# Loads moved to other places in the order, keys in whole rows, and 64 bytes between the squares and the weights

## The chip, the cores and the metric

The kernel runs on one core of one Trainium2 chip. A core has five engines with a queue each: TensorE (PE; the loading of its stationary operand is shown apart, as PEld), VectorE (DVE), ScalarE (ACT), GpSimd (POOL) and SyncE (SP), which here issues every transfer. The engines work in the order of their own queues and wait for each other through semaphores. The metric is the time of one execution on the device in microseconds (us); lower is better.

## The reference

Attention with a local window and block summaries, and a feed-forward layer behind it, all in float32:

```python
k_sum = k.reshape(B, H, nb, block, D).max(axis=3)      # B, H, S, D = 4, 8, 768, 64; block 32
v_sum = v.reshape(B, H, nb, block, D).mean(axis=3)     # nb = 24
scores_l = scale * q @ k^T, kept where |i - j| < 16, else -1e9
scores_s = scale * q @ k_sum^T + log(32)
a = softmax([scores_l, scores_s])
attn = a @ [v, v_sum]
x = attn as 3072 tokens x 512
out = square(max(x @ w_in, 0)) @ w_out                 # 512 -> 2048 -> 512
```

## The kernel before

**Groups and chunks.** The 3072 tokens are 24 groups `g` of 128 (six to a batch, `NT = 6`); group `g` belongs to batch `g // 6`. Two groups make a chunk `c` of 256 tokens, and there are 12 chunks. The feed-forward layer of a chunk walks the 2048 hidden features in 16 blocks of 128, two to a slot.

**The feed-forward layer.** Every float32 operand is split in a high and a low part of type float32r, and a product is made of three: high by high, low weights by high, high weights by low. `ffn1` (L391) makes 12 matmuls for one block: the stationary operand is a piece of the weights `w_sb[f]`, the moving one is `xh` or `xl`, 256 columns. `squares` applies ReLU (ACT, L399), the high square `gh` (ACT, L405), the product (DVE, L410) and the low square `gl` (DVE, L413). `ffn2` (L432) makes 6 matmuls for one block: the stationary operand is a piece of the squares `gh_sb` or `gl_sb`, the moving one is 512 columns of `w_sb[f]`. A slot, so, is 24 matmuls of L391 and 12 of L432; the second product of a slot comes after the first product of the next slot (`finish`).

**Attention's visits.** While TensorE works on chunk `c`, the softmax of the groups of the next chunk runs on DVE, ACT and POOL. `period(a)` lists that work for the groups `a` and `a + 1` over eight slots; each slot has three lists, `before` and `after` the squares and `last`. At the end of its eighth list, `last[7]`, stands what this text calls a visit: TensorE leaves the feed-forward layer and makes `outputs(a)` and `outputs(a + 1)` (L361, 32 matmuls) and then `scores_by_group(a + 2)` (L278, 128 matmuls, for two groups). `split_x` then makes `xh` and `xl` of the next chunk. One slot of the running chunk follows the visit before the next chunk begins.

**Loads.** All transfers are issued by SP, in the order of the program. `load_v` (L139), `load_q` (L125) and `load_k` (L131, L132) of the groups to come stand in `last[7]`, right behind the visit in the order: values for `a + 2` and `a + 3`, queries and keys for `a + 4` and `a + 5`. As SP has its own queue, it issues them as soon as the buffers are free, which two matmul groups of the visit decide: `outputs` for the values, `scores_by_group` for the queries and keys. Buffers go by `g % 2`. `load_kv` (L175, L176) brings whole rows of keys and values of the next batch, out of which `sum_k` (L179) and `sum_v` (L184, L187) make the block maxima and means on DVE; it stands in `last[0]` and `last[3]`, the sums two slots later.

**The keys' layout.** In `k_sb` a row (one partition) holds 8 runs of 120 elements: 64 keys, the 24 block maxima, 32 keys. A load fills the keys of each run (256 bytes and 128 bytes a piece, two transfers) and leaves the 24 maxima alone. `place_k` (L191) copies the maxima out of `ksum` on DVE, four times in the opening and once for each of two groups at the turn of a batch; the copy then serves the batch.

**Memory.** Tiles of the pool `const` lie one after the other in the order of the code, then the pool `big` with 17 rooms of 8192 bytes a partition (the weights, and the rows of `load_kv` in the one spare), then `work` with three `nmx` and three `sm` tiles of 32 bytes each, `xh`, `xl` and the output tiles. `gh_sb` and `gl_sb` (4096 bytes each) are the last of `const`, so that they begin a whole multiple of 256 bytes before every room of the weights.

**The order.** The string `START` is the order of the opening, written by hand, up to about 140 us; behind it `slot` and `period` give it for the chunks 2 to 11. No planner moves anything.

Of the kernel before, what the change touches and what calls it, by code (L numbers as in the profile page):

```python
# [11 lines left out]
F32 = mybir.dt.float32  # L12
# [5 lines left out]
ALU = mybir.AluOpType  # L18
AX = mybir.AxisListType

B, H, S, D = 4, 8, 768, 64
BLOCK, WINDOW = 32, 16
NB = S // BLOCK
DM, DF = 512, 2048
P = 128
NT = S // P
NPAIR = H // 2
# [6 lines left out]
NK = 96 + NB  # L34
GQ = 32
GK = 64 + NB
FROM_GROUPS = 6
# [36 lines left out]
def attn_ffn_kernel(ctx: ExitStack, tc: tile.TileContext, q, k, k0, kt, v, vt, v0, w, masks, gmasks, ident, mean, out):  # L74
    nc = tc.nc
    scale = 1.0 / math.sqrt(D)

    const = ctx.enter_context(tc.tile_pool(name="const", bufs=1))
# [14 lines left out]
    k_sb = [const.tile([P, 2 * NPAIR * NK], F32, name=f"k_sb{i}") for i in range(2)]  # L93
# [4 lines left out]
    def by_pair(g):  # L98
        return k_sb[g % 2].rearrange("a (s p k) -> a s p k", s=2, p=NPAIR)
# [4 lines left out]

    e_sb = const.tile([P, H, P], F32, name="e_sb")
    pT = [const.tile([P, H, P], F32, name=f"pT{i}") for i in range(2)]
    ksum = const.tile([P, NPAIR, NB], F32, name="ksum")
    vsum = const.tile([P, NPAIR, 32], F32, name="vsum")
    r_sb = const.tile([P, 2, CT], F32, name="r")
    gh_sb = const.tile([P, 4, CT], F32R, name="gh")  # L110
    gl_sb = const.tile([P, 4, CT], F32R, name="gl")


    bank = [ps_s.tile([P, DM], F32, name=n, tag=f"{n}{i}") for i, n in enumerate(["s_ps"] * 4 + ["ph"] * 2)]
# [12 lines left out]
    def load_k(g):  # L127
        if g < FROM_GROUPS:
            nc.sync.dma_start(out=by_run(g)[:, 0:4], in_=k0[g - FROM_KT])
        else:  # L130
            nc.sync.dma_start(out=by_pair(g)[:, :, :, 0:64], in_=k[g // NT, g % NT][:, :, :, 0:64])  # L131
            nc.sync.dma_start(out=by_pair(g)[:, :, :, GK:], in_=k[g // NT, g % NT][:, :, :, 64:])  # L132

    def load_qk(g):
        load_q(g)
        load_k(g)

    def load_v(g):
        nc.sync.dma_start(out=v_sb[g % 2][0:96], in_=v[g // NT, g % NT])  # L139
# [21 lines left out]
    kv, padded = {}, {}  # L161
# [11 lines left out]
    def load_kv(b, p):  # L173
        kv[b, p] = r = room(F32, "kv")
        nc.sync.dma_start(out=r[:, 0:S], in_=kt[b, p])  # L175
        nc.sync.dma_start(out=r[:, S : 2 * S], in_=vt[b, p])  # L176

    def sum_k(b, p):
        nc.vector.tensor_reduce(  # L179
            out=ksum[:, p], in_=kv[b, p][:, 0:S].rearrange("a (n j) -> a n j", j=BLOCK), op=ALU.max, axis=AX.X  # L180
        )

    def sum_v(b, p):
        nc.vector.tensor_reduce(  # L184
            out=vsum[:, p, 0:NB], in_=kv[b, p][:, S : 2 * S].rearrange("a (n j) -> a n j", j=BLOCK), op=ALU.add, axis=AX.X
        )
        nc.vector.tensor_scalar_mul(vsum[:, p, 0:NB], vsum[:, p, 0:NB], 1.0 / BLOCK)  # L187

    def place_k(g):
        dst = by_run(g)[:, 4] if g < FROM_GROUPS else by_pair(g)[:, :, :, 64:GK]  # L190
        nc.vector.tensor_copy(out=dst, in_=ksum.unsqueeze(1).to_broadcast([P, 2, NPAIR, NB]))  # L191

    def place_v(g):
        dst = v_sb[g % 2][96:128]
# [88 lines left out]
    def scores_kt(g, p0, p1):  # L283

        if g not in s_ps:
            s_ps[g] = [bank[r].rearrange("a (p k) -> a p k", p=NPAIR) for r in range(2)]
        for p in range(p0, p1):
            for k0, k1 in ((0, 96), (96, NK)):
                for r, s in ((0, 0), (1, 1), (0, 1), (1, 0)):
                    rs, ss = slice(r * 64, r * 64 + 64), slice(s * 64, s * 64 + 64)  # L290
                    o = g * P + s * 64
                    keys = ksum[rs, p, :] if k0 else padded[p // 2][rs, p % 2, o : o + 96]
                    nc.tensor.matmul(  # L293
                        s_ps[g][r][ss, p, k0:k1], lhsT=q_sb[g % 2][rs, s, p, :], rhs=keys, start=True, stop=True
                    )
# [56 lines left out]
    x_ps = {}  # L352

    def outputs(g):
        xp = bank[2 if g < FROM_GROUPS - 1 else 5 if g < FROM_GROUPS else 5 - g % 2]
        x_ps[g] = xp = xp.rearrange("a (p k) -> a p k", p=NPAIR)

        for s in range(2):
            for h in range(H):
                o = (h % 2) * 64  # L360
                nc.tensor.matmul(  # L361
                    xp[o : o + 64, h // 2, s * 64 : s * 64 + 64],
                    lhsT=v_sb[g % 2][:, s, h * 64 : h * 64 + 64],
                    rhs=pT[g % 2][:, h, s * 64 : s * 64 + 64],
                    start=True, stop=True,
                )
# [13 lines left out]
    def split_x(g):  # L380
        high_x(g)
        low_x(g)
# [71 lines left out]
    n_g = B * NT  # L454
# [28 lines left out]
    def period(a):  # L483

        before, after, last = [[] for _ in range(8)], [[] for _ in range(8)], [[] for _ in range(8)]
        b, t = divmod(a, NT)
        if a >= n_g:  # L490
            return before, after, last
        if b and t == 0:
            after[1] += [lambda: place_v(a), lambda: place_v(a + 1)]
        after[0].append(lambda: softmax(a, 0, 3))
        before[1].append(lambda: softmax(a, 3, 6))
        after[1] += [lambda: softmax(a, 6, 8), lambda: inverse(0), lambda: norm(a, 0, nc.gpsimd)]
        before[2] += [lambda: inverse(1), lambda: norm(a, 1, nc.gpsimd)]
        after[2].append(lambda: turn(a, 0, 3))
        before[3].append(lambda: turn(a, 3, 8))
        after[3].append(lambda: turn(a, 8, 12))  # L500
        before[4].append(lambda: softmax(a + 1, 0, 4))
        after[4].append(lambda: softmax(a + 1, 4, 6))
        before[5] += [lambda: softmax(a + 1, 6, 8), lambda: inverse(0), lambda: norm(a + 1, 0, nc.gpsimd)]
        before[5] += [lambda: inverse(1), lambda: norm(a + 1, 1, nc.gpsimd)]
        before[6].append(lambda: turn(a + 1, 0, 5))
        after[6].append(lambda: turn(a + 1, 5, 8))
        before[7].append(lambda: turn(a + 1, 8, 12))
        if b + 1 < B and t:
            for n, p in enumerate(((0, 1), (2, 3))[t // 4]):
                last[3 * n].append(lambda p=p: load_kv(b + 1, p))  # L510
                after[3 * n + 2].append(lambda p=p: sum_k(b + 1, p))
                after[3 * n + 2].append(lambda p=p: sum_v(b + 1, p))
        if b + 1 < B and t == 4:
            after[6] += [lambda: place_k(a + 2), lambda: place_k(a + 3)]
        last[7] += [lambda: outputs(a), lambda: outputs(a + 1)]
        if a + 2 < n_g:
            last[7].append(lambda: scores_by_group(a + 2))
        last[7] += [lambda: split_x(a), lambda: split_x(a + 1)]
        if a + 2 < n_g:
            last[7] += [lambda g=g: load_v(g) for g in (a + 2, a + 3)]  # L520
        if a + 4 < n_g:
            last[7] += [lambda g=g: load_qk(g) for g in (a + 4, a + 5)]
        return before, after, last


# [3 lines left out]
    free, held = [3, 4, 5], {}  # L529
# [93 lines left out]
    with tc.manual_schedule(engines=None):  # L623
        for token in START.split():
            what, i, j, eng = re.fullmatch(r"(L:[a-z]+|F[12]|[A-Z]+)\.?(\d*)\.?(\d*)([avp]?)", token).groups()
            i, j = int(i or 0), int(j or 0)
# [10 lines left out]
        for c in range(2, n_c):  # L637
            for f in range(0, NF, 2):
                n = (f + 2) // 2 % 8
# [37 lines left out]
def _layouts(q, k, v):  # L677
    qd = q.reshape(B, NPAIR, 2, NT, 2, 64, D).transpose(0, 3, 2, 6, 4, 1, 5)
    kp = np.zeros((B, H, S + 2 * WINDOW, D), k.dtype)
    kp[:, :, WINDOW : WINDOW + S] = k  # L680
    vp = np.zeros((B, H, S + 2 * WINDOW, D), v.dtype)
    vp[:, :, WINDOW : WINDOW + S] = v
    kd = np.zeros((B, NT, 2, D, 2, NPAIR, 96), k.dtype)
    vd = np.zeros((B, NT, 96, 2, H, D), v.dtype)
    for s in range(2):
        for t in range(NT):
            o = t * P + s * 64
            kd[:, t, :, :, s] = kp[:, :, o : o + 96].reshape(B, NPAIR, 2, 96, D).transpose(0, 2, 4, 1, 3)
            vd[:, t, :, s] = vp[:, :, o : o + 96].transpose(0, 2, 1, 3)
    return {  # L690
        "q": np.ascontiguousarray(qd).reshape(B, NT, P, 2, NPAIR, 64),
        "k": kd.reshape(B, NT, P, 2, NPAIR, 96),
        "k0": np.ascontiguousarray(
            kd[0, FROM_KT:].reshape(FROM_GROUPS - FROM_KT, P, 2, NPAIR, 4, NB).transpose(0, 1, 4, 2, 3, 5)
        ),
        "kt": np.ascontiguousarray(k.transpose(0, 1, 3, 2)).reshape(B, NPAIR, P, S),
        "v": vd.reshape(B, NT, 96, 2, DM),
        "vt": np.ascontiguousarray(v.transpose(0, 1, 3, 2)).reshape(B, NPAIR, P, S),
        "v0": np.ascontiguousarray(v[0].reshape(H, NT, P, D).transpose(2, 1, 0, 3)).reshape(P, NT, DM),
    }  # L700
# [24 lines left out]
```

## Time and profile before

| what | value |
|---|---|
| time, median of 3 runs (lowest to highest) | 635.54 us (632.82 to 636.05) |
| the profiled execution: its own time | 633.53 us |
| its span, first to last instruction | 631.7 us |
| TensorE busy (matmul) | 601.6 us, 95% of the span |
| weight load busy | 545.1 us, 86% |
| DVE, ACT, POOL busy | 385.4, 262.5, 88.8 us |
| mean granted TensorE clock | 0.986 |
| moved by DMA | 60.56 MB in 55104 packets |

A busy share says how long an engine had work, not that the work was needed at that time. The chain of waits goes back from the last instruction to what released it, and so on to the start; its pieces are a start, a length and what ran. A piece called issue is time in which the engine waited for nothing that the profile shows. The view by stretches gives, for each stretch of time, the busy time of each engine with its number of instructions, the granted clock of TensorE, the share of the 16 DMA engines in use, and GB/s.

### The profile page before, as it was taken

The page shows a single profiled execution, that of the slowest core. Times are in us where ns is not written, and L with a number is a line of the kernel's source. Part 1 is how long each engine was busy: PE and PEld are TensorE (multiplying, and loading weights), DVE is VectorE, ACT ScalarE, POOL GpSimd, SP SyncE. Part 2 cuts the span into 40 slices and gives each one's busy share as a digit, 9 for nine tenths or more (in the row PEclk, how much of TensorE's full clock was granted, in tenths as well). Part 3 has the DMA queues.
Part 4 walks back from the last instruction along what each step waited for, and adds up shares of the span by engine and source line. Part 5 has one row for each costly group of instructions (what it writes and reads, how often), then busy time and mean ns, then how long its engine had stood idle before and what let it go on. Part 6 is the DMA issues. An engine that isn't in the chain of part 4 may idle for free.

```text
span 631.7 us, 14142 instructions
## 1 busy us (share of the span) xinstructions
PE 601.6 (95%) x5792; PEld 545.1 (86%) x5792; DVE 385.4 (61%) x1077; ACT 262.5 (42%) x690; POOL 88.8 (14%) x83
## 2 busy tenths in 40 slices
PE   3689999999989999999999998999999999999997
PEld 2588889989979999999989988998998998998996
DVE  4889888668535755756644772783763663653221
ACT  3778887332424324424424423334433423332222
POOL 2555663002000000002000000000200000000000
PEclk9879999999999999999999998999999999999999
DMA  8999611553043134123026115205005001000000
GB/s 290 381 341 317 212 71 52 166 164 90 1 111 110 49 87 132 51 76 93 1 58 162 51 38 148 84 1 135 35 1 135 34 0 52 34 2 1 34 1 33
DMA packets 55104, 60.56 MB, mean 96 GB/s; under 512 B 40320, under 2 KB 40448, under 8 KB 52992
## 3 DMA queue, kind: packets, MB, share of 16 engines
q1 hardware_dynamic: 55040, 59.67, 31.5%
q8 instruction: 45, 0.74, 0.5%
q14 instruction: 19, 0.16, 0.1%
HBM read 53.36 MB, written 6.29 MB: 94 GB/s over the span
## 4 chain that ended last, share of the span: by engine, by line
PE 91%; DMA 4%; DVE 2%; issue 1%; SPq 1%; ACT 0%; DVEq 0%
PE ph L391 41%; PE o_ps L432 41%; DMA w_raw<-in_w 4%; PE ph L361 3%; PE s_ps L391 3%; PE s_ps L278 2%; DVE w_raw L236 1%; PE s_ps L361 1%; PE ph L336 0%; PE s_ps L293 0%; PE s_ps L261 0%; DVE w_sb L247 0%; SPq L171 0%; DVE sm L323 0%; ACT w_raw L225 0%
## 5 line engine op out<-in xcount | busy, mean ns | idle before, releaser
L391 PE MATMUL ph<-xh,w_sb 128*128 128x256 f32 x1448 | 264.2, 284 | 2.8 <-issue 2.2
L391 PEld LDWEIGHTS ph<-xh,w_sb 128*128 128x128 f32 x1448 | 228.9, 190 | 10.7 <-issue 2.4
L432 PE MATMUL o_ps<-w_sb,gh 128*128 128x512 f32 x768 | 237.2, 390 | 0.0
L391 PE MATMUL ph<-xl,w_sb 128*128 128x256 f32 x724 | 204.6, 283 | 0.0
L410 DVE TENSOR_TENSOR ph<-ph,r 128x512 f32<-128x512 f32 (+1 forms) x101 | 64.9, 643 | 160.5 <-ACT r L399 159.2
L432 PEld LDWEIGHTS o_ps<-w_sb,gh 128*128 128x128 f32 x768 | 137.3, 188 | 22.8 <-issue 0.2
L432 PE MATMUL o_ps<-w_sb,gl 128*128 128x512 f32 x384 | 149.7, 390 | 0.9 <-DVE gl L413 0.9
L399 ACT ACTIVATE r<-ph 128x512 f32<-128x512 f32 (+1 forms) x91 | 52.0, 571 | 226.0 <-PE ph L391 225.1
L391 PEld LDWEIGHTS ph<-xl,w_sb 128*128 128x128 f32 x724 | 140.1, 194 | 0.0
L314 ACT ACTIVATE e_sb<-e_sb,nmx 128x88 f32<-128x88 f32 (+1 forms) x192 | 69.9, 367 | 71.3 <-DVE nmx L306 71.3
L347 DVE STREAM_TRANSPOSE pT<-e_sb 32x256 f32<-32x256 f32 x216 | 94.1, 436 | 3.4 <-POOL e_sb L330 0.4
L432 PEld LDWEIGHTS o_ps<-w_sb,gl 128*128 128x128 f32 x384 | 72.1, 188 | 16.4 <-DVE gl L413 1.3
L330 POOL TENSOR_TENSOR e_sb<-e_sb,sm 128x352 f32<-128x352 f32 (+1 forms) x43 | 34.7, 810 | 336.4 <-DVE sm L324 198.4
L413 DVE TENSOR_TENSOR gl<-ph,gh 128x512 fp32r<-128x512 f32 (+1 forms) x101 | 64.3, 637 | 10.5 <-DVE ph L410 0.5
L405 ACT ACTIVATE gh<-r 128x512 fp32r<-128x512 f32 (+1 forms) x112 | 64.0, 571 | 9.3 <-DVE r L401 5.8
L240 POOL TENSOR_TENSOR w_raw<-w_raw 128x1024 int32<-128x1024 int32 x16 | 35.6, 2233 | 25.4 <-DVE w_raw L236 8.7
L314 ACT ACTIVATION_READ_ACCUMULATOR e_sb<-e_sb,nmx 128x1 f32 x192 | 36.4, 190 | 0.0
L306 DVE CUSTOM_DVE_ANT_0 e_sb<-s_ps,gmask_sb 128x88 f32<-128x88 f32 x144 | 27.1, 244 | 0.4
L378 DVE TENSOR_TENSOR xl<-ph,xh 128x512 fp32r<-128x512 f32 x19 | 13.1, 691 | 22.4 <-ACT xh L375 22.4
L323 DVE TENSOR_SCALAR sm<-sm 128x4 f32<-128x4 f32 x48 | 13.4, 280 | 16.0 <-ACT e_sb L314 16.0
L375 ACT CAST xh<-ph 128x512 fp32r<-128x512 f32 x19 | 11.1, 587 | 26.6 <-PE ph L361 26.6
L361 PEld LDWEIGHTS ph<-pT,v_sb 128*64 128x64 f32 x608 | 18.6, 138 | 3.8 <-issue 3.2
(66 smaller groups left out, 391.3 us busy)
## 6 DMA issues: line engine op xcount, KB each, us to landing
w_raw<-in_w SPq DMA_DIRECT2D x16, 1024.0 KB, 14.9
v_sb<-in_v SPq DMA_DIRECT2D x24, 384.0 KB, 4.9
kv<-in_kt SPq DMA_DIRECT2D x16, 384.0 KB, 3.4
q_sb<-in_q SPq DMA_DIRECT2D x24, 256.0 KB, 5.3
out<-ob SPq DMA_DIRECT2D x24, 256.0 KB, 2.1
k_sb<-in_k SPq DMA_DIRECT2D x18, 256.0 KB, 5.1
kv<-in_vt SPq DMA_DIRECT2D x12, 384.0 KB, 3.9
k_sb<-in_k SPq DMA_DIRECT2D x18, 128.0 KB, 5.2
```

Of the source, the lines that this page charges most:

```text
L240: nc.gpsimd.tensor_tensor(out=hi, in0=hi, in1=lo, op=ALU.add)
L306: nc.vector.tensor_tensor_reduce(out=e_sb[:, h, 0:n], in0=s_ps[g][h % 2][:, h // 2, 0:n], in1=m, scale=-scale, scalar=3.0e38, op0=ALU.add, ...
L314: nc.scalar.activation(e, e, AF.Exp, bias=nmx[half][:, i : i + 1], scale=-1.0, accum_out=sm[half][:, i : i + 1])
L330: eng.tensor_mul(out=e, in0=e, in1=sm[half].unsqueeze(2).to_broadcast([P, 4, n]))
L347: nc.vector.transpose(out=pT[g % 2][j * 32 : j * 32 + 32, :, i * 32 : i * 32 + 32], in_=e_sb[i * 32 : i * 32 + 32, :, c : c + 32],)
L361: nc.tensor.matmul(xp[o : o + 64, h // 2, s * 64 : s * 64 + 64], lhsT=v_sb[g % 2][:, s, h * 64 : h * 64 + 64], rhs=pT[g % 2][:, h, s * 64 ...
L391: nc.tensor.matmul(ph, lhsT=w_sb[f][:, w, cc * P : (cc + 1) * P], rhs=x[c][:, cc, :], start=(n == 0), stop=(n == 3 * NC4 - 1))
L399: nc.scalar.activation(r, ph, AF.Relu)
L405: nc.scalar.activation(gh, r, AF.Square)
L410: nc.vector.tensor_mul(out=ph, in0=ph, in1=r)
L413: nc.vector.tensor_sub(out=gl, in0=ph, in1=gh.bitcast(F32))
L432: nc.tensor.matmul(o_ps[c][tt], lhsT=g_[:, ts_], rhs=w_sb[f][:, w, DM:], start=(first and n == 0), stop=(last and n == 2),)
```

## The change

Five things are changed.

- The tile `ksum` becomes two tiles by the parity of the batch, and a tile `gap` of 64 bytes comes after `gl_sb`. The squares then begin 8256 bytes before the first room of the weights instead of 8192, that is 192 bytes past a multiple of 256.
- Keys are laid out on the host in whole rows of 960 elements, with zeros at the 24 places of each run where the maxima go; a load is one transfer of 3840 bytes a partition. As it overwrites the maxima, `place_k` follows every load; in the periods it runs on ACT, in `after[5]` and `after[6]`.
- The loads leave `last[7]`: values of `a` and `a + 1` go to `last[1]` of the period that uses them, queries and keys of `a + 2` to `last[1]` and of `a + 3` to `last[3]`.
- The second `load_kv` of a period goes from `last[3]` to `last[2]`, its sums from `after[5]` to `after[4]`.
- `outputs(5)` takes the first bank of the list `free` instead of bank 5. By the order of `START` the list stands at 5, 4, 3 there, so that it is the same bank.

```diff
-    ksum = const.tile([P, NPAIR, NB], F32, name="ksum")
+    ksums = [const.tile([P, NPAIR, NB], F32, name=f"ksum{i}") for i in range(2)]
...
     gl_sb = const.tile([P, 4, CT], F32R, name="gl")
+    const.tile([P, 16], F32, name="gap")
...
-            nc.sync.dma_start(out=by_pair(g)[:, :, :, 0:64], in_=k[g // NT, g % NT][:, :, :, 0:64])
-            nc.sync.dma_start(out=by_pair(g)[:, :, :, GK:], in_=k[g // NT, g % NT][:, :, :, 64:])
+            nc.sync.dma_start(out=k_sb[g % 2], in_=k[g // NT, g % NT])
...
-    def place_k(g):
+    def place_k(g, eng=nc.vector):
         dst = by_run(g)[:, 4] if g < FROM_GROUPS else by_pair(g)[:, :, :, 64:GK]
-        nc.vector.tensor_copy(out=dst, in_=ksum.unsqueeze(1).to_broadcast([P, 2, NPAIR, NB]))
+        copy(eng, dst, ksums[g // NT % 2].unsqueeze(1).to_broadcast([P, 2, NPAIR, NB]))
...
-        xp = bank[2 if g < FROM_GROUPS - 1 else 5 if g < FROM_GROUPS else 5 - g % 2]
+        xp = bank[2 if g < FROM_GROUPS - 1 else free[0] if g < FROM_GROUPS else 5 - g % 2]
...
+        if a > FROM_GROUPS:
+            last[1] += [lambda: load_v(a), lambda: load_v(a + 1)]
...
-                last[3 * n].append(lambda p=p: load_kv(b + 1, p))
-                after[3 * n + 2].append(lambda p=p: sum_k(b + 1, p))
-                after[3 * n + 2].append(lambda p=p: sum_v(b + 1, p))
-        if b + 1 < B and t == 4:
-            after[6] += [lambda: place_k(a + 2), lambda: place_k(a + 3)]
+                last[2 * n].append(lambda p=p: load_kv(b + 1, p))
+                after[2 * n + 2].append(lambda p=p: sum_k(b + 1, p))
+                after[2 * n + 2].append(lambda p=p: sum_v(b + 1, p))
+        if a + 3 < n_g:
+            for n, g in enumerate((a + 2, a + 3)):
+                if g > 9:
+                    last[2 * n + 1].append(lambda g=g: load_qk(g))
+                after[n + 5].append(lambda g=g: place_k(g, nc.scalar))
         last[7] += [lambda: outputs(a), lambda: outputs(a + 1)]
         if a + 2 < n_g:
             last[7].append(lambda: scores_by_group(a + 2))
         last[7] += [lambda: split_x(a), lambda: split_x(a + 1)]
-        if a + 2 < n_g:
-            last[7] += [lambda g=g: load_v(g) for g in (a + 2, a + 3)]
-        if a + 4 < n_g:
-            last[7] += [lambda g=g: load_qk(g) for g in (a + 4, a + 5)]
...
+    kg = np.zeros((B, NT, 2, D, 2, NPAIR, NK), k.dtype)
...
+    kg[..., 0:64], kg[..., GK:] = kd[..., 0:64], kd[..., 64:]
...
-        "k": kd.reshape(B, NT, P, 2, NPAIR, 96),
+        "k": kg.reshape(B, NT, P, 2 * NPAIR * NK),
```

More of the change, by code (lines that the diff above doesn't have):

```diff
@@ L179, in sum_k @@
         nc.vector.tensor_reduce(
-            out=ksum[:, p], in_=kv[b, p][:, 0:S].rearrange("a (n j) -> a n j", j=BLOCK), op=ALU.max, axis=AX.X
+            out=ksums[b % 2][:, p], in_=kv[b, p][:, 0:S].rearrange("a (n j) -> a n j", j=BLOCK), op=ALU.max, axis=AX.X
         )
@@ L291, in scores_kt @@
                     o = g * P + s * 64
-                    keys = ksum[rs, p, :] if k0 else padded[p // 2][rs, p % 2, o : o + 96]
+                    keys = ksums[0][rs, p, :] if k0 else padded[p // 2][rs, p % 2, o : o + 96]
                     nc.tensor.matmul(
```

## The prediction

> **What bounds the kernel now.** I read the shares of the engines first, then the chain of waits, then the same chain period by period.
>
> ```profile
> PE 601.6 (95%) x5792; PEld 545.1 (86%) x5792; DVE 385.4 (61%) x1077; ACT 262.5 (42%) x690; POOL 88.8 (14%) x83
> PE 91%; DMA 4%; DVE 2%; issue 1%; SPq 1%; ACT 0%; DVEq 0%
> PE ph L391 41%; PE o_ps L432 41%; DMA w_raw<-in_w 4%; PE ph L361 3%; PE s_ps L391 3%; PE s_ps L278 2%; DVE w_raw L236 1%; PE s_ps L361 1%; PE ph L336 0%; PE s_ps L293 0%; PE s_ps L261 0%; DVE w_sb L247 0%; SPq L171 0%; DVE sm L323 0%; ACT w_raw L225 0%
> ```
>
> TensorE is the bound: two lines of the feed-forward layer hold 82% of the chain. What can be won is either TensorE's idle time or the time of one matmul. The small entry "issue" matters, as it is TensorE waiting for nothing that is shown. The stretches that follow run from the same place of one period to that of the next, each with one visit in it:
>
> ```profile
> 190.55:238.73 48.18, 48.18 (x482) 43.96 (x482) 30.69 (x89) 17.97 (x54) 3.10 (x4) 1.00 0.29 80
> 238.73:286.83 48.10, 48.10 (x482) 43.87 (x482) 31.13 (x91) 17.95 (x54) 3.11 (x4) 1.00 0.32 88
> 286.83:335.92 49.09, 48.31 (x482) 43.88 (x482) 28.40 (x87) 18.16 (x54) 4.79 (x7) 1.00 0.24 61
> 335.92:388.61 52.69, 50.07 (x482) 45.63 (x482) 30.73 (x91) 18.01 (x54) 3.10 (x4) 0.97 0.37 100
> 388.61:436.71 48.10, 48.10 (x482) 43.88 (x482) 31.09 (x91) 17.99 (x54) 3.10 (x4) 1.00 0.22 64
> 436.71:485.06 48.35, 48.35 (x482) 44.02 (x482) 28.41 (x89) 18.19 (x54) 4.79 (x7) 1.00 0.23 60
> 485.06:534.00 48.94, 48.48 (x483) 44.07 (x482) 26.78 (x83) 18.00 (x54) 3.10 (x4) 1.00 0.12 35
> ```
>
> The work is the same in all seven, 482 matmuls, and the time is not: 48.10 at best, 52.69 at worst. The chain shows where. An undisturbed visit first, then the first and the worst one:
>
> ```profile
> 277.55 2.02 PE ph L361 x64
> 279.57 1.59 PE s_ps L278 x113
> 281.16 2.93 PE ph L391 x24
> 284.09 2.73 PE o_ps L432 x12
> ...
> 178.92 2.02 PE ph L361 x64
> 183.08 2.17 issue
> 187.81 2.73 PE o_ps L432 x12
> ...
> 378.31 2.62 issue
> 381.28 4.57 PE ph L391 x24
> 385.84 2.77 PE o_ps L432 x12
> ...
> 328.89 0.78 issue
> 527.08 0.46 issue
> ```
>
> A visit packs 192 pairs of weight load and matmul into 3.6 us (277.55 to 281.16), where a slot has 36 pairs in 5.56 us (2.73 in the row of 284.09, and 2.83 in a row quoted further down). The four stalls come in visits one, four, five and eight. Instructions reach an engine by DMA, and the page lists that as a queue of its own:
>
> ```profile
> q8 instruction: 45, 0.74, 0.5%
> ```
>
> 45 packets of 0.74 MB for 2 x 5792 instructions are one packet of 16.4 KB for each 257 instructions. A period of 964 instructions is 3.75 packets, so that the border of a packet comes to the same place of a visit every fourth visit: the spacing of the stalls (one and five, four and eight). And what else is moving then:
>
> ```profile
> 229.00:231.50 2.50, 2.50 (x83) 2.13 (x89) 0.38 (x1) 0.65 (x2) 0.00 (x0) 1.00 0.02 5
> 377.00:379.50 2.50, 1.31 (x117) 1.13 (x97) 0.87 (x2) 0.39 (x1) 0.00 (x0) 1.00 0.90 265
> 382.00:384.50 2.50, 2.50 (x14) 2.50 (x14) 0.00 (x0) 0.00 (x0) 0.00 (x0) 0.50 0.83 187
> 375.86 1.26 SPq L139 DMA_DIRECT2D v_sb<-in_v  x2
> 378.66 1.27 SPq L132 DMA_DIRECT2D k_sb<-in_k  x1
> ```
>
> The DMA engines are idle until the visit frees the values' buffers (0.02 busy in 229.00:231.50), and 0.90 busy in the worst stall. My reading is that the next packet of instructions stands in line with the loads that the visit itself has set off. After the stall of 2.62 us the granted clock is 0.50, and the 24 matmuls at 381.28 take 4.57 instead of 2.93.
>
> [...]
>
> **The change part by part.** *Loads out of the visit.* The seven periods are over 48.10 by 0.08 + 0 + 0.99 + 4.59 + 0 + 0.25 + 0.84 = 6.75. The first visit takes 8.89 from its start to the second product (178.92 to 187.81) against 6.54 (277.55 to 284.09): 2.35. Together 9.10, the clock's loss included. Without loads beside it the fetch still takes some time and the visit is as dense; what can stay is bounded by nothing and by the smallest stall shown in each of four visits, 4 x 0.46 = 1.84. I take one, 0.46: gain 8.64.
>
> *Where the loads go.* In slot 1, values, queries and keys of `a + 2` are queued on SP behind the output stores and the first `load_kv`; in slot 3 the queries and keys of `a + 3` behind the second `load_kv`, which waits for the sums of the first.
>
> ```profile
> v_sb<-in_v SPq DMA_DIRECT2D x24, 384.0 KB, 4.9
> kv<-in_kt SPq DMA_DIRECT2D x16, 384.0 KB, 3.4
> k_sb<-in_k SPq DMA_DIRECT2D x18, 256.0 KB, 5.1
> SPq L175 <- DVE vsum L184: 27.5, 4, 7.0
> SPq L450 <- ACT ob L121: 137.9, 14, 46.0
> ```
>
> The values are wanted six slots on (33 us), the keys' copies four slots on (22 us, `a + 2`) and three (17 us, `a + 3`). Landing takes about 5, the longest wait of `load_kv` is 7.0: 0. If the cover were gone, ACT would stand at the copy with the next ReLU behind it. A transfer of keys in whole rows moves 480 KB, between 3.4 (whole rows, 384 KB) and 5.1 us (the pieces); either end is covered. A fetch that such a load delays by the same 5 us in a slot finds 72 instructions a slot used: 257 last three and a half slots, 0.
>
> *Copies of the maxima.* Eight copies on DVE become four there and sixteen on ACT (eight periods of two).
>
> ```profile
> L191 DVE COPY k_sb<-ksum 128x192 f32<-128x192 f32 x8 | 1.9, 256 | 0.1
> L314 ACT ACTIVATE e_sb<-e_sb,nmx 128x88 f32<-128x88 f32 x144 | 51.3, 358 | 59.3 <-DVE nmx L306 59.3
> L399 ACT ACTIVATE r<-ph 128x256 f32<-128x256 f32 x11 | 4.3, 389 | 7.4 <-PE ph L391 6.5 <-DVE gl L413 0.6 <-ACT e_sb L314 0.3
> ACT r L399 <- PE ph L391: 225.1, 71, 8.5
> ```
>
> 192 columns on ACT lie between 358 and 389 ns; 16 x 0.37 = 5.9 us, beside 225 us in which ACT waits for TensorE: 0, and up to 5.9 if it were not hidden.
>
> *Sums a slot earlier.* The same work on DVE, now further ahead of the visit; DVE is 61% busy: 0. The doubled `ksum` takes away a wait in the opening that the chain does not show: 0. The bank of `outputs(5)` is the same.
>
> *Squares 192 bytes on.* No row of this kernel has the squares there, so bounds.
>
> ```profile
> 232.99 3.02 PE ph L391 x24
> 238.73 2.83 PE ph L391 x24
> ```
>
> The same 24 matmuls after a visit take 2.93 at 281.16 and 3.02 at 232.99 (no stall in either), 4 ns apart each. So matmuls of one form do run at more than one pace, and an address could decide which. 2.83 / 24 is 118 ns for 256 columns, 2.73 / 12 is 227 ns for 512, or 114 for 256: the product with squares is the quicker one by column. Gains: if the 2304 matmuls of L391 (96 slots of 24) went to the quicker pace, 96 x 0.09 = 8.6 us; the 96 groups of 12 of L432 have no quicker pace in the trace. Loss: `xh` lies 192 bytes past a multiple of 256 from the weights already (six tiles of 32 bytes stand ahead of it), and its matmuls are those of 118 ns; at that pace L432 takes 2 x 118 = 236 instead of 227, 1152 x 9 = 10.4 us. Between these ends I take 0: of two lines that differ in length, operands and place, the rows can't say which is due to the place.
>
> [...]
>
> **The sum.** 633.53 (the profiled execution) - 8.64 = 624.9. The median of the runs is 2.0 above that execution and the runs lie 3.2 apart; if that is stalls falling differently, they go too, so I do not add it.
>
> **The rivals.**
>
> *The place of the squares helps.* For it: two paces of the same instruction, and the faster one seen only behind visits, so that it is not a matter of the data. Against: L391's operands stay where they are to each other; only what the squares leave behind could set its pace. Price: up to 8.6 more, 616.3.
>
> *The stalls stay.* The dense visit itself, not the loads, empties TensorE's instructions. For it: the rhythm of the packets would be there without any load. Against: a stall of 0.46 in one visit and of 2.62 in another asks for something beside the density, which is the same in all. Then of the 9.10 the four stalls (2.17 + 2.62 + 0.78 + 0.46 = 6.03) and the slow clock (4.57 - 2.93 = 1.64) stay: 633.53 - 9.10 + 7.67 = 632.1. The loads' doing less than they say (the first `load_kv` still comes one slot behind a visit) ends there too.
>
> *The place of the squares hurts.* The stationary squares and the moving weights then collide as the pair of L391 does: 236 ns each. The visits' gain holds: 624.9 + 10.4 = 635.3, slower than 633.53 by 1.8. It decides from 8640 / 1152 = 7.5 ns a matmul. For it: the one pair that lies so is the slower by column. Against: 118 also fits a fixed cost for each matmul, which weighs double where matmuls are half as long.
>
> *A new wait.* The copies on ACT come late behind SP and hold the ReLU: up to 5.9, 630.8. By the rows there are 12 us of cover (17 less 5).
>
> **How the numbers follow.** The forecast of 624.9 has 0.50, the squares' help 0.25, stalls that stay 0.09, the squares' harm 0.10, the new wait 0.06. The likeliest case alone lies between 623.5 (all 9.10 and 1 us of scatter) and 627. The range reaches down past 616.3 to 612, as L432 might gain with L391, and up to 632, which takes in the new wait and the edge of the stalls that stay. A measurement of this kernel tells apart about 0.5%, 3.2 us. Faster by more than that, below 632.3: all of the first two, the new wait and half of the stalls' case, 0.86. Within it: the rest of that case and two thirds of the harm, 0.11. Slower: 0.03.
>
> **What would show it.** Right: no issue piece over 0.3 us in any visit, periods of 48.1 with L391 at 2.83 and L432 at 2.73, DMA share near 0 in the visits and moved into slots 1 and 3, ACT's copies with no wait for DMA that holds a ReLU. Wrong: stalls of the same rhythm with idle DMA engines (the second rival), groups of 24 or 12 at another time than 2.83 and 2.73 (the squares), or a wait of ACT L399 that ends with a copy. A result over 632 or under 616 would mean that the pace of the matmuls moved.

## The result and the profile after

The changed kernel takes 624.67 us (median of 4 runs, 622.87 to 626.05); the kernel before, beside it, 634.18 (632.44 to 636.05). The ratio is 0.985, with an interval of 0.983 to 0.988: 9.5 us off. The profiled execution has 623.76 against 633.53.

The line numbers of the changed kernel are one higher: L391 is L392, L432 is L433, L361 is L362, L278 is L279. One thing of the counts: a product of float32 operands in attention shows as two pairs of weight load and matmul. A visit's outputs are 32 calls and show as 64 pairs, its scores are 64 calls (not 128) and show as 128 pairs: the 192 of the prediction.

First three periods of the changed kernel, an undisturbed one and two with a stall, from the second slot behind one visit to the same place behind the next. The columns are start and end, length, busy time and number of instructions of PE, PEld, DVE, ACT and POOL, granted clock, DMA share and GB/s.

```profile
187.85:235.60 47.75, 47.75 (x483) 43.35 (x482) 30.91 (x89) 18.45 (x55) 3.10 (x4) 1.00 0.30 94
283.35:331.97 48.62, 47.95 (x483) 43.35 (x482) 28.40 (x87) 18.63 (x56) 4.78 (x7) 1.00 0.22 76
331.97:381.25 49.28, 48.04 (x482) 43.46 (x482) 30.94 (x89) 18.50 (x56) 3.10 (x4) 1.00 0.29 91
```

Two things are to be seen. The undisturbed period is 47.75 and no longer 48.10, so the work itself got shorter. And the other two are still over it, by 0.87 and 1.53; before it was 0.99 and 4.59. The chain of waits of the changed kernel shows both:

```profile
193.34 2.75 PE ph L392 x24
196.09 2.75 PE o_ps L433 x12
...
181.53 0.88 issue
182.41 2.64 PE ph L392 x21
...
325.05 0.67 issue
...
374.00 1.24 issue
375.57 2.93 PE ph L392 x24
...
518.38 0.18 issue
```

The groups of 24 went from 2.83 to 2.75, those of 12 from 2.72 to 2.75 (the 2.73 of the prediction's row stands right behind a visit; most rows before have 2.72, as `226.66 2.72 PE o_ps L432 x12`); the stalls of the visits from 2.17, 0.78, 2.62 and 0.46 to 0.88, 0.67, 1.24 and 0.18, so from 6.03 to 2.97, in the same four visits. Behind the worst one the 24 matmuls take 2.93 where they took 4.57 (at a granted clock of 1.00 instead of 0.50). What stands beside those stalls now, in the view by stretches:

```profile
180.00:182.50 2.50, 1.62 (x94) 1.40 (x77) 0.69 (x1) 0.02 (x1) 0.00 (x0) 1.00 0.00 0
324.00:326.50 2.50, 1.83 (x130) 1.50 (x109) 0.94 (x2) 0.46 (x1) 0.00 (x0) 1.00 0.00 0
372.50:375.00 2.50, 1.50 (x125) 1.31 (x121) 1.05 (x2) 0.57 (x1) 0.00 (x0) 1.00 0.04 10
```

The DMA engines are idle, and TensorE stalls all the same. Taken over the four stalls alone, from their start to their end, the DMA share is 0.00 in each; before it was 0.97, 0.78, 0.99 and 0.79. The account of the 9.77 between the two profiled executions: stalls 6.03 - 2.97 = 3.06; the slow clock 4.57 - 2.93 = 1.64; the pace, 96 slots of 2.83 + 2.72 - 2.75 - 2.75 = 0.05, 4.8, or 5.2 with the 0.054 that the last seven undisturbed slots give without rounding. Together 9.5 to 9.9. That it closes so well is partly chance: the slot right behind a visit gains nothing (2.93 and 2.73 before, 2.93 and 2.75 after), and the opening, whose slots hold other work too, is counted as if it were all such slots.

Of the smaller parts, the copies of the maxima, the sums and the loads, the page and the views of the changed kernel say:

```profile
L123 ACT COPY k_sb<-ksum 128x192 f32<-128x192 f32 x16 | 5.4, 335 | 0.0
k_sb<-in_k SPq DMA_DIRECT2D x18, 480.0 KB, 6.1
DMA packets 20256, 62.33 MB, mean 100 GB/s; under 512 B 3168, under 2 KB 3296, under 8 KB 18144
ACT r L400 <- PE ph L392: 206.3, 72, 5.5
```

Sixteen copies of 335 ns, none behind an idle ACT; the ReLU waits for TensorE alone, 206 us of it. A load of keys in one piece takes 6.1 us to land where the pieces took 5.1 and 5.2 each, and the packets fall from 55104 to 20256.

### The profile page after: what moved, and what is told of

It reads as the page before. It is cut to its first block, busy times and chain, and to the rows that moved or that the text cites. A ratio compares the mean times of both kernels' runs of the same rounds, so it can differ in the third digit from the quotient of the medians.

```text
span 622.0 us, 14129 instructions
## 1 busy us (share of the span) xinstructions
PE 595.3 (96%) x5792; PEld 536.8 (86%) x5792; DVE 385.8 (62%) x1073; ACT 266.5 (43%) x706; POOL 89.4 (14%) x83
## 4 chain that ended last, share of the span: by engine, by line
PE 91%; DMA 3%; DVE 2%; ACT 1%; issue 1%; SPq 1%; POOL 0%; DVEq 0%; POOLq 0%
PE o_ps L433 41%; PE ph L392 40%; PE ph L362 3%; PE s_ps L279 2%; PE s_ps L392 2%; DMA w_raw<-in_w 2%; DMA q_sb<-in_q 2%; PE ph L337 1%; PE s_ps L294 1%; PE s_ps L362 1%; DVE w_sb L248 0%; PE o_ps L149 0%; ACT w_sb L123 0%; PE s_ps L262 0%; SPq L172 0%
## 5 line engine op out<-in xcount | busy, mean ns | idle before, releaser
L392 PE MATMUL ph<-xh,w_sb 128*128 128x256 f32 x1448 | 255.8, 279 | 1.5 <-issue 0.9
L433 PE MATMUL o_ps<-w_sb,gh 128*128 128x512 f32 x768 | 238.0, 391 | 0.0
L392 PEld LDWEIGHTS ph<-xh,w_sb 128*128 128x128 f32 x1448 | 225.5, 189 | 9.8 <-issue 1.1
L392 PE MATMUL ph<-xl,w_sb 128*128 128x256 f32 x724 | 201.1, 278 | 0.0
L433 PEld LDWEIGHTS o_ps<-w_sb,gh 128*128 128x128 f32 x768 | 137.1, 188 | 24.8 <-issue 0.2
L433 PE MATMUL o_ps<-w_sb,gl 128*128 128x512 f32 x384 | 151.4, 394 | 0.8 <-DVE gl L414 0.8
L392 PEld LDWEIGHTS ph<-xl,w_sb 128*128 128x128 f32 x724 | 136.7, 189 | 0.0
L433 PEld LDWEIGHTS o_ps<-w_sb,gl 128*128 128x128 f32 x384 | 72.3, 188 | 15.6 <-DVE gl L414 1.3
L324 DVE TENSOR_SCALAR sm<-sm 128x4 f32<-128x4 f32 x48 | 14.9, 311 | 14.7 <-ACT e_sb L315 14.6
L362 PEld LDWEIGHTS ph<-pT,v_sb 128*64 128x64 f32 x608 | 18.6, 138 | 3.9 <-issue 3.3
```

The source lines that it names most:

```text
L362: nc.tensor.matmul(xp[o : o + 64, h // 2, s * 64 : s * 64 + 64], lhsT=v_sb[g % 2][:, s, h * 64 : h * 64 + 64], rhs=pT[g % 2][:, h, s * 64 ...
L392: nc.tensor.matmul(ph, lhsT=w_sb[f][:, w, cc * P : (cc + 1) * P], rhs=x[c][:, cc, :], start=(n == 0), stop=(n == 3 * NC4 - 1))
L433: nc.tensor.matmul(o_ps[c][tt], lhsT=g_[:, ts_], rhs=w_sb[f][:, w, DM:], start=(first and n == 0), stop=(last and n == 2),)
```

## The experiments

**The two causes apart.** The place of the squares alone, put into the kernel before:

```diff
     gl_sb = const.tile([P, 4, CT], F32R, name="gl")
+    const.tile([P, 16], F32, name="gap")
```

> The kernel before, and nothing but the tile of 64 bytes that puts the squares 192 bytes past a multiple of 256 from the weights. Theory A (place and loads are two causes that add): the groups of 24 of L391 go from 2.83 to 2.75 us and the groups of 12 of L432 from 2.73 to 2.75, 0.06 a slot, so about 5.5 us off: some 628.5; the stalls of the visits stay as they were, 2.2, 0.8, 2.6 and 0.5 us in visits one, four, five and eight. Theory B (the quicker pace comes from fewer DMA packets beside the matmuls, the place does nothing): 2.83 and 2.73 as before, 633 to 635.

Measured 627.04 (624.85 to 629.51), ratio 0.987 (0.984 to 0.991). In the chain of its profiled execution (629.51):

```profile
191.12 2.75 PE ph L392 x24
193.87 2.75 PE o_ps L433 x12
182.14 2.11 issue
184.25 4.07 PE ph L392 x21
328.59 0.63 issue
377.49 2.84 issue
523.77 0.63 issue
```

The pace is the changed kernel's, the stalls (6.21) are those of before, and a slow clock follows the first of them (0.50 granted in 185.00:187.50, 21 matmuls in 4.07).

The loads alone, so the changed kernel without the tile:

```diff
-    const.tile([P, 16], F32, name="gap")
```

> The changed kernel without the tile of 64 bytes: loads moved, keys in whole rows, copies on ACT, the squares a whole multiple of 256 bytes from the weights. Theory A: groups back at 2.83 and 2.73, stalls of the visits as in the changed kernel (0.9, 0.7, 1.2, 0.2, sum 3.0 against 6.0), clock near 0.99: 629 to 630. Theory B: 2.75 and 2.75, and the whole gain is here: 624 to 625.

Measured 628.48 (627.42 to 629.68), ratio 0.991 (0.989 to 0.993); the profiled execution has 628.56. In its chain:

```profile
188.64 2.83 PE ph L391 x24
191.47 2.72 PE o_ps L432 x12
182.17 1.07 issue
327.00 0.67 issue
376.31 1.50 issue
522.10 0.41 issue
```

Pace of before, stalls 3.65. Theory A holds in both: the pace belongs to the place and not to the number of packets, the shorter stalls to the loads. (The loads' new places, the whole rows and the copies on ACT stand together in this run; no run parts them.) In the profiled executions the two parts are 4.02 and 4.97, and both together 9.77. By the medians they are 7.3 and 5.9 against 9.5 together; the runs of the first lie 4.7 apart, and I can't say whether there is more behind that than the fall of the clock in one run and not in another (its mean is 0.989 in the run of 629.51, 0.991 or 0.992 in the other three).

**What the rest of the stalls is.** Half a packet of instructions more in the opening:

```diff
-    def scores_by_group(g):
+    def scores_by_group(g, groups=None):
...
-        for t in (g, g + 1):
+        for t in groups or (g, g + 1):
...
+        scores_by_group(6, (6,))
         load_v(6)
```

> The changed kernel with the scores of group 6 made twice in the opening: 64 more pairs of weight load and matmul, 128 instructions, half of a packet of instructions; the second result is the same as the first. Theory A (stalls come where the border of a packet falls in a visit): the border moves by half a packet, which is two visits on in the rhythm of four, so the stalls go from visits one, four, five and eight to visits two, three, six and seven. Theory B (they belong to what those visits do, or to the batch): they stay in one, four, five and eight. The time is the changed kernel's, 624, plus 1 us for the pairs.

The chain of waits around its visits two, three, six and seven:

```profile
233.98 0.71 issue
282.96 1.56 issue
429.76 0.42 issue
478.59 1.02 issue
```

The other four visits have no stall. The visits do the same work as before at the same place in the batch, and only their place in the instruction stream has moved; so the stall belongs to the border of a packet of instructions.

The trace lists every packet of the instruction queue with its start and length, and this settles what a stall ends on. In all 49 stalls of this kind, in the twelve profiled executions that have any, TensorE goes on 1.2 to 1.6 us after such a packet has landed (in the worst one before, the packet moves from 378.55 to 379.47 and TensorE goes on at 380.94; in the changed kernel from 372.76 to 373.90, and at 375.24). It shows the part of the loads too. In visits one and five the packet set out 3.84 and 3.81 us behind the visit's start before the change, and 2.29 and 2.34 after it; those stalls are 1.29 and 1.38 shorter. In visits four and eight it had set out before the visit's loads did, 1.48 and 1.04 behind the start (now 1.35 and 0.98), and those stalls are only 0.11 and 0.28 shorter.

Without loads the length goes by how late in the visit the border comes. By the pieces of the chain behind the stalls, `518.57 0.73 PE s_ps L279 x38` and `375.24 0.34 PE s_ps L279 x3` in the changed kernel, the stall is 0.18 with 38 of the scores' matmuls still to come and 1.24 with 3; in this run it is 0.42 with 36 and 1.02 with 6.

The 632.45 of that run is more than expected. Besides the pairs it met a new stall in the opening, where the 64 pairs make that place denser, and a slow clock behind it (0.54 granted in 142.50:145.00; the row of 142.87). And from its third visit to its sixth the slots ran at another pace, 0.10 longer, though no operand had moved:

```profile
140.78 2.08 issue
142.87 4.32 PE ph L392 x23
...
290.28 2.83 PE ph L392 x24
293.11 2.77 PE o_ps L433 x12
...
436.57 2.75 PE ph L392 x24
```

If a dense visit runs out of fetched instructions, thinner visits should not stall. Scores one slot ahead of the outputs:

```diff
-                after[n + 5].append(lambda g=g: place_k(g, nc.scalar))
+                after[5].append(lambda g=g: place_k(g, nc.scalar))
...
         if a + 2 < n_g:
-            last[7].append(lambda: scores_by_group(a + 2))
+            last[6].append(lambda: scores_by_group(a + 2))
```

> The changed kernel with the scores of the next two groups one slot earlier than the outputs, so that a visit's 192 pairs come in two lots of 128 and 64 with 36 pairs of the feed-forward layer between; both copies of the maxima stand in the sixth slot. Theory A (the stalls that are left are TensorE running out of fetched instructions in a dense visit): no stall in any visit, 3.0 us off, less what one more change between attention and the feed-forward layer costs in eight periods (up to 0.25 each, 2.0): 621.5 to 624.5. Theory B (the scores themselves wait for something, buffers or banks): the stalls stay inside the scores, and the time is 625 or more.

Measured 626.46 (625.68 to 626.86), ratio 0.988 (0.986 to 0.990), so 1.8 above the changed kernel by the medians. No stall is left in the visits, as theory A has it. Its time, 621.5 to 624.5, did not come, as another wait took what was won. One visit of the chain:

```profile
228.65 1.11 PE ph L362 x32
229.78 0.59 ACT xh L376
230.39 0.70 DVE xl L379
```

The outputs use the two banks of the feed-forward layer's first product, and without scores behind them the next product stands until the split has read the bank (4.3 us in nine waits). So a third order: outputs of the first group three slots earlier, in a bank that its softmax has left; scores behind the seventh slot; outputs of the second group behind the eighth, in the bank that the next product does not want.

```diff
-        xp = bank[2 if g < FROM_GROUPS - 1 else free[0] if g < FROM_GROUPS else 5 - g % 2]
+        xp = bank[2 if g < FROM_GROUPS - 1 else free[0] if g < FROM_GROUPS else 4 * (g % 2)]
...
-                after[n + 5].append(lambda g=g: place_k(g, nc.scalar))
-        last[7] += [lambda: outputs(a), lambda: outputs(a + 1)]
+                after[5].append(lambda g=g: place_k(g, nc.scalar))
+        last[4] += [lambda: outputs(a), lambda: split_x(a)]
         if a + 2 < n_g:
-            last[7].append(lambda: scores_by_group(a + 2))
-        last[7] += [lambda: split_x(a), lambda: split_x(a + 1)]
+            last[6].append(lambda: scores_by_group(a + 2))
+        last[7] += [lambda: outputs(a + 1), lambda: split_x(a + 1)]
```

> The changed kernel with a visit in three lots: outputs of the first group behind the fifth slot, in a bank that its own softmax has left, with its split into xh and xl there; scores of the next two groups behind the seventh; outputs of the second group and its split behind the eighth, in the bank that the next first product does not use. Both copies of the maxima in the sixth slot. Theory A (dense visits run out of fetched instructions, and what the visit in two lots gave back was the wait of the next product for the split): no issue stall and no wait for the split, in the last visit neither; 3.0 us of stalls and 1.4 us of the last visit off, about 0.06 for each of 17 more changes (1.0) back: 621 to 622. Theory B (the stalls are a fixed cost of attention's matmuls wherever they stand): 624.7 or more.

Measured 625.13 (624.63 to 625.91), ratio 0.988 (0.985 to 0.991): not told apart from the changed kernel. The stalls are gone, as theory A has it, and the time is theory B's. The two periods that were read out are alike now, 48.38 each, with TensorE busy all through. One of them:

```profile
210.50:258.88 48.38, 48.38 (x482) 43.33 (x481) 30.52 (x89) 18.41 (x54) 3.10 (x4) 1.00 0.28 92
```

48.38 is 0.63 above the undisturbed 47.75: two more changes between attention and the feed-forward layer cost 0.3 each, not 0.06, and what the stalls had taken (2.97 in eight visits, 0.37 a period) is spent on them. The first 24 matmuls behind a lot take 2.93 to 3.02 instead of 2.75. So the stalls that are left can be removed, and by these orders there is nothing to win.

**How far the place goes.** Is it the address itself or the distance? The tile of 64 bytes ahead of everything moves the squares, and leaves the weights and `xh` where the changed kernel has them:

```diff
+    const.tile([P, 16], F32, name="gap")
     mask_sb = const.tile([P, 3, NK], F32, name="mask_sb")
...
-    const.tile([P, 16], F32, name="gap")
```

> The changed kernel with the tile of 64 bytes ahead of all tiles: every address is as in the changed kernel from the weights on, the squares lie 64 bytes further, a whole multiple of 256 from the weights. Theory A (the distance between the two operands of a matmul decides): groups of 24 and 12 at 2.83 and 2.72, as without the tile. Theory B (where the weights or xh themselves lie decides): 2.75 and 2.75.

627.89, and the groups are those of distance 0:

```profile
187.68 2.83 PE ph L392 x24
190.51 2.72 PE o_ps L433 x12
```

So the place of the weights or of `xh` alone does not decide, as both lie where the changed kernel has them. Nor does the squares' own address, which the changed kernel and the run without the tile have in common. A distance does. L392 does not read the squares, and still its pace goes with them (2.83 here, 2.75 in the changed kernel).

Other distances, all by the size of the tile (8, 24, 32 and 48 elements in place of 16):

> The changed kernel with a tile of 128 bytes instead of 64: squares 128 bytes past a multiple of 256 from the weights. Theory A (any distance that is no multiple of 256 does): 2.75 and 2.75. Theory B (192 is one of few): other times, between 2.72 and 2.83 for either group.

> The changed kernel with a tile of 192 bytes: squares 64 bytes past a multiple of 256 from the weights, the mirror of 192. Theory A (any distance that is no multiple of 256 does): 2.75 and 2.75. Theory B (192 is one of few): other times, between 2.72 and 2.83 for either group.

> The changed kernel with a tile of 32 bytes: squares 224 bytes past a multiple of 256 from the weights. A slot (24 of L392 and 12 of L433) took 5.55 us at 0, 5.49 at 192, 5.55 at 128 and 5.58 at 64 in the runs before this. Theory A (the distance counts in steps of 64 bytes): 224 is as 192, 5.49 (2.75 and 2.75). Theory B (it counts finer): another time, between 5.44 (2.72 and 2.72) and 5.58.

> The changed kernel with a tile of 96 bytes: squares 160 bytes past a multiple of 256 from the weights. Theory A (steps of 64 bytes): as 128, 5.55 a slot with 2.83 and 2.73 in turn for L392 and 2.78 for L433. Theory B (finer): another time.

And `xh` and `xl` moved instead, by a tile ahead of theirs (16 and 48 elements), the squares staying at 192:

```diff
+    work.tile([P, 16], F32, name="xgap", tag="xgap", bufs=1)
```

> The changed kernel with 64 bytes more ahead of the pool that holds xh and xl, so that these begin a whole multiple of 256 bytes from the weights instead of 192 past it; squares as in the changed kernel. Theory A (for each product the distance of its own two operands sets the pace): L392, whose operands moved, goes to what L433 had at distance 0, 2.72 for 24 (113 ns each), L433 stays at 2.75: 5.47 a slot, 1.9 us off in all. Theory B (the pace is a state that one product hands on to the next, and only the pair of distances counts): both groups change, to no time that can be read from one pair.

> The changed kernel with 192 bytes more ahead of the pool that holds xh and xl, so that these begin 128 bytes past a multiple of 256 from the weights (192 in the changed kernel, 0 in the run before this); squares as in the changed kernel. Theory A (0 is bad for x as any crowding of the two reads is, and places away from 0 are alike): 2.75 and 2.75, 624 to 625. Theory B (only the pair of distances counts, as x at 0 slowed both groups to 2.88 and 2.75): another pair of times, a slot between 5.44 (2.72 and 2.72, 620) and 5.63 (637).

The first theory of each of these six runs failed: not every distance does, steps finer than 64 count, and with `xh` moved neither 2.72 nor 2.75 came for L392. The groups of 24 and of 12 in the chains of these kernels (one line number higher in the two with `xh` moved), with the profiled executions' own times (the last is a median of ten runs, ratio 1.003, 1.001 to 1.006):

| squares past 256 | x past 256 | 24 of L392 | 12 of L433 | a slot | time, us |
|---|---|---|---|---|---|
| 0 (loads alone) | 192 | 2.83 | 2.72 | 5.55 | 628.56 |
| 64 | 192 | 2.83 and 2.74 in turn | 2.79, 2.80 | 5.58 | 632.57 |
| 128 | 192 | 2.83 and 2.73 in turn | 2.78 | 5.56 | 630.06 |
| 160 | 192 | 2.75 | 2.80 | 5.55 | 629.34 |
| 192 (the changed kernel) | 192 | 2.75 | 2.75 | 5.50 | 623.76 |
| 224 | 192 | 2.83 | 2.80 | 5.63 | 636.58 |
| 192 | 0 | 2.88 | 2.75 | 5.63 | 636.50 |
| 192 | 128 | 2.88, in two periods 2.84 | 2.76 | 5.64 | 635.07 |

Rows from the chains of 128 and 224 for the squares, and of 0 for x:

```profile
189.16 2.83 PE ph L392 x24
191.98 2.78 PE o_ps L433 x12
194.76 2.73 PE ph L392 x24
...
195.99 2.83 PE ph L392 x24
198.82 2.80 PE o_ps L433 x12
...
196.02 2.88 PE ph L393 x24
198.90 2.75 PE o_ps L434 x12
```

The slot explains the time: 224 is 0.13 a slot above the changed kernel, times 96 is 12.5, and 623.76 + 12.5 = 636.3 against 636.58. Finer than 64 it does matter (224 is not 192, 160 is not 128), and no order can be read from one product alone: with x at 0, L392 does not take the 113 ns that L433 has at 0, it slows to 120 (2.88 / 24). Of the eight pairs tried the changed kernel's is the quickest. Others were not tried. Two things limit what the table says. A third distance goes with the two, that of the squares from `xh` (the first column less the second); it is 0 in the changed kernel alone, and no run parts it from the others. And five of the rows rest on one execution each, while at one and the same distance a slot took 5.50 or 5.60 (the run with half a packet more).

## Why the prediction was right, and where it was not

The time, 624.9 against 624.67, and the direction were right; the likeliest case as it was written was not. Its sum holds one term that was too large, by about 4 us, and one that was missing, of 4 to 5 us. That they cancel to 0.2 us is luck.

*Loads out of the visit: 8.64 forecast, 4.7 found* (3.06 of stalls and 1.64 of clock; 4.97 by the profiled execution with the loads alone). Reckoned as the prediction reckoned it, the periods over the undisturbed one and the first visit, 9.10 became 4.00. The reading behind it held: packets of instructions of 16.4 KB, borders that come back to the same place of a visit at every fourth, a packet that sets out behind the visit's own loads (3.84 and 3.81 behind the start of visits one and five, 2.29 and 2.34 without those loads). The step that failed is the bound on what stays without loads: four times 0.46, as if the smallest stall were the fetch's own. The changed kernel leaves 2.97 with idle DMA engines. The second rival (the dense visit itself) is half of the truth, and its 6.03 of stalls shares out as about half to either cause. The objection to it, that the density is the same in all visits and the stalls are not, failed: with idle DMA engines they still go from 0.18 to 1.24, by where in the visit the border comes. And the stalls go with the stream of instructions: half a packet more moved them by two visits.

*Squares 192 bytes on: 0 forecast, 4 to 5 found* (4.02 by the place alone, 4.80 between the loads alone and the changed kernel, 4.8 to 5.2 by the pace). The first rival was right in kind: matmuls of L391 did go to a quicker pace, 96 x 0.08 = 7.7, close to the 8.6 that it gave as its most, and L432 gave back 96 x 0.03 = 2.9. The objection to it, that L391's operands stay where they are to each other, was true and did not count: the pace went with the squares all the same. By what way is open. A loss of the size that was given, 10.4, was not far off either: at distance 224 a slot takes 5.63 where it takes 5.55 at 0, 7.7 more in 96 slots. The argument by likeness with `xh`, from which the 236 ns of the third rival came, is refuted: at 192 the squares' product takes 2.75 / 12 = 229 ns. That the two operands of L391 collide, as that rival has it, no run shows.

*The rest* went as written in time: the copies on ACT (335 ns each, under the 358 to 389 that were given), the sums a slot earlier and the later loads cost nothing that the chain shows; no ReLU waits for a copy. Whole rows of keys landed in 6.1 us, a little outside the 3.4 to 5.1 given, well inside the cover of 17. The signs named for the right case (no issue piece over 0.3 us, groups at 2.83 and 2.73) did not come; those for the second rival and for the squares both did.

## What to carry to other kernels

A stall that the profile puts down to nothing is worth a division of instructions by packets of the instruction queue: if it returns with the period of the packets, look for a dense stretch of short instructions and keep transfers away from it (here that took the stalls from 6.03 to 2.97 us), and price the rest before breaking the stretch up, as each change of work cost too (0.3 us here). Where matmuls set the time, compare the pace of one and the same form over the trace. Where it has two values at the same clock, as here 2.83 and 2.75 for 24 matmuls of one line at 1.00, the distance between the operands in memory is a cheap thing to try: here it moved a slot between 5.50 and 5.64 us. Change one of two edits at a time before believing either: a sum that comes out right can hold two wrong terms.

## What was not expected of the hardware

The pace is a state that lasts. The kernel with visits in three lots runs its slots at 2.83 and 2.77 from the opening to its first visit, and at 2.75 and 2.75 behind it, with the operands at the same distances:

```profile
149.86 2.83 PE ph L392 x24
152.69 2.77 PE o_ps L433 x12
...
167.81 2.75 PE ph L392 x24
170.55 2.75 PE o_ps L433 x12
```

The run with half a packet more goes into that slower state behind its third visit and out of it behind its sixth (the rows of 290.28 and 436.57); both times attention's matmuls stand between. At distances 64 and 128 the pace of L392 goes to and fro from slot to slot. What one matmul hands on to the next, no run here shows.

The granted clock does not follow the length of a stall alone: it fell behind one of 2.11 and not behind one of 2.84 in the same execution (the place of the squares alone). In these traces it changes in steps of 3.41 us: each fall behind a stall lasts 3.41, and all its other whole stretches are multiples of that. The step before the fall, then the two in which the stall of 2.84 lies (the figure behind the length is TensorE's busy time):

```profile
180.66:184.07 3.41, 1.48 (x85) 1.27 (x68) 0.66 (x1) 0.00 (x0) 0.00 (x0) 1.00 0.89 263
375.22:378.63 3.41, 2.27 (x151) 2.02 (x146) 1.38 (x2) 1.00 (x2) 0.00 (x0) 1.00 0.71 197
378.63:382.04 3.41, 1.71 (x15) 1.57 (x15) 0.00 (x0) 0.00 (x0) 0.00 (x0) 1.00 1.13 227
```

TensorE stood idle for 1.93 us of the first step, and for 1.14 and 1.70 of the others. In the other two falls behind a stall it was 2.47 (the kernel before) and 1.93 (the run with half a packet more). Behind stalls, so, the clock fell after steps with 1.93 to 2.47 idle and not after those with 1.14 and 1.70. No fixed limit comes out of that, as in the opening it also fell behind steps with only 1.50 (distance 128) and 1.51 (the kernel before) idle.
